# Another order of loads, scans and decode beside the first token tile, and a fifth decay buffer

## The chip, the cores and the metric

The kernel runs on one core of a Trainium2 chip. The metric is the device time of one execution in microseconds. The core has five engines with a queue of instructions each: TensorE (PE in the profile, with PEld for its weight loads), VectorE (DVE), ScalarE (ACT), GpSimd (POOL) and SyncE (SP), which here issues every transfer. Each engine takes its own queue in order.

## What is computed

Three layers follow one another. The first is a scan attention with decays over 4 batches of 8 heads, 768 positions, head size 32 and state size 16:

```
for each chunk c:
    cum = cumsum(log a);  L = exp(cum_i - cum_j), i >= j
    y   = (C B^T * L) x  +  (C state) * exp(cum)
    state = exp(sum log a) * state + sum_j B_j x_j exp(cum_end - cum_j)
```

Its output, as 3072 tokens of 256, goes through two feed-forward layers in float32:

```
h   = max(x w1, x w2, x w3);            x = h w_out      (256 -> 768 -> 256)
out = (sigmoid(x w_gate) * (x w_val)) w_out2             (256 -> 1536 -> 256)
```

## The kernel before

**Attention.** Chunks have 96 positions. A chunk is 8 *steps* (k = 8c + g) of four (batch, head) units; 32 units make 8 steps, so there are 64 steps. A step multiplies C and B (tile s, L320 in the first 16 steps, L323 behind), multiplies the result by the decays (tile mt: odd steps and the first four on VectorE, L335; even ones copied by ScalarE, L331, and multiplied on GpSimd, L332), puts B times the last decay beside it (GpSimd, L328) and multiplies by x (tile y, L341), which gives the output and the new state at once. Every fourth step, ScalarE casts y into xt_hi (L350), VectorE takes the remainder as xt_lo (L352) and transposes the new state into the next chunk's x (L356, four instructions).

**Decays.** One tile dec holds the decays of two steps. It is loaded by a broadcast transfer from a clipped copy in DRAM (load_decay, L255) and turned into running products by two scans on VectorE (decay, L271). Four buffers hold such tiles. So decays n serve steps 2n and 2n + 1.

**B and C from chunk 2 on** come as three bfloat16 parts (split_bc, L282): ScalarE casts, GpSimd subtracts, and twelve transfers put the parts in place.

**Weights of layer one** come as 64-bit words in twelve *pieces*, two for each of six column groups (a00, a01, a10, ... are pieces 0, 1, 2, ...). Decode (L152) makes float32 of a piece and splits it: three operations on ScalarE (L164 to L167), t_a and r_a on VectorE (L171, L173), a cast on ScalarE (L199) and a subtraction on GpSimd (L201). The table BEHIND says how many pieces are loaded right behind the decays of a number.

**Token tiles.** Layer one works on tiles of 512 tokens. The first needs steps 0 to 11 (START = 12). Each of its six groups makes three products u in three PSUM banks (L390 to L392; L391 reads xt_lo), whose maximum ScalarE and VectorE take (L457, L459, L461), and then the products o of the group before. Between the groups, 12 more steps of attention are fed in.

**Order.** The instructions are traced by generators in a Pipe, whose ticks fix the program's order; a planner then lays each engine's queue, by program order among what its own timing model holds ready. `issue_after(i)` adds an edge that keeps an instruction behind i on i's engine. What sets the order around the change is prepare(k) (L361), which is called in step k and issues loads, scans and the parts of the split, and the lines from L486 on.

Of the kernel before, what the change touches and what calls it, by code (L numbers as in the profile page):

```python
# [8 lines left out]
F32 = mybir.dt.float32  # L9
# [6 lines left out]
ALU = mybir.AluOpType  # L16
# [3 lines left out]
CH = 96  # L20
NC = S // CH
NU = NB * NH
NG = NU // 4
# [9 lines left out]
LW = CH + 1  # L33
PU = 8
NP = NU // PU

BW = 4 * 128
# [6 lines left out]
MASKED = 8  # L44
LEAD = 2
MTS = 5
DECS = 4
UNTIL = [12, 24, 36, 50, 64, 64, 64]
SLOT = {1: 0, 2: 1, 6: 3, 5: 4, 7: 6, 3: 2, 4: 5}
WEIGHT = {1: 0, 2: 2, 3: 1, 4: 3, 5: 4, 6: 5, 7: 6}  # L50

BEHIND = {4: 1, 5: 1, 6: 2, 7: 2, 8: 2, 9: 1, 10: 1, 11: 1, 12: 1}


class Pipe:
# [15 lines left out]
def scan_attention_then_ffn(ctx: ExitStack, tc: tile.TileContext, xh, ah, bch, pick, bn, w1, w2, w3,  # L71
# [62 lines left out]

    todo = [(piece1, m, part) for m in range(M1) for part in range(2)]
    loaded = []

    sgs = [stp.tile([128, DEC // 128, 128], I32, tag=f"sg{k}", bufs=1, name=f"sg{k}") for k in range(2)]
    blocks_done = []
    for sg in sgs:  # L140
        pool.memset(sg, 0)

    def load_weights():

        f, m, part = todo.pop(0)
        wpool, blocks, loads, name = f(m, part)
        raw = wpool.tile([128, 2 * len(loads), 128, 2], I32, tag=name, name=f"raw_{name}")
        for k, s in enumerate(loads):
            sp.dma_start(out=raw[:, 2 * k:2 * k + 2].rearrange("p b n t -> p b (n t)"), in_=s)
        loaded.append((raw, wpool, blocks, name))  # L150

    def decode(raw, wpool, blocks, name):  # L152
        nb = raw.shape[1]
        second = name[0] != "a"

        def behind(k):
            return tc.issue_after(evict[k].ins) if second else ExitStack()

        f1 = raw[..., 1]
        r = stp.tile([128, DEC // 128, 128], I32, tag="r", bufs=3, name=f"r_{name}")[:, 0:nb]  # L160
        sg = sgs[len(blocks_done) % len(sgs)][:, 0:nb]
        blocks_done.append(name)
        with behind(0):
            act.activation(out=sg.bitcast(F16).rearrange("p b (n t) -> p b n t", t=2)[..., 1], in_=f1.bitcast(F32),  # L164
                           func=AF.Identity, scale=2.0 ** -112)
            act.mul(f1.bitcast(F32), f1.bitcast(F32), 2.0 ** -112)
            act.mul(r, raw[..., 0].bitcast(U32), 2.0 ** -29)  # L167
        yield
        t = stp.tile([128, DEC // 128, 128], I32, tag="t", bufs=2, name=f"t_{name}")[:, 0:nb]
        with behind(1):  # L170
            dve.scalar_tensor_tensor(out=t, in0=f1, scalar=3, in1=sg, op0=ALU.logical_shift_left,  # L171
                                     op1=ALU.bitwise_or)
            dve.tensor_tensor(out=r, in0=t, in1=r, op=ALU.add)  # L173
        yield
        if second:
            hi, lo = store2(wpool, blocks, name)
            parts = [(r.bitcast(F32), slice(0, 4))]
            if name[0] != "d":
                v = r.bitcast(F32)
                q = wq[0].tile([128, 3, 128], F32, tag="q", name=f"q_{name}")  # L180
# [20 lines left out]
        pool.tensor_tensor(out=w[:, 1], in0=r.bitcast(F32), in1=w[:, 0].bitcast(F32),  # L201
                           op=ALU.subtract)

    def weights_tick(last=True):
        if loaded and last:
# [14 lines left out]
    def constants():  # L220
# [4 lines left out]
        for r in range(4):  # L225
# [8 lines left out]
        act.copy(delta, delta_s)  # L234

    dec, xs, cs, bx = {}, {}, {}, {}

# [16 lines left out]

    def load_decay(n, src):  # L255
        t = awk.tile([128, PU, LW], F32, tag="dec", bufs=DECS, name=f"dec{n}")
        i = sp.dma_start(out=t.rearrange("p u w -> p (u w)"), in_=src[n].partition_broadcast(128))
        dec[n] = t
        for _ in range(BEHIND.get(n, 0)):
            with tc.issue_after(i.ins):  # L260
                load_weights()

    def load_x(c, part=slice(0, NU)):
        if c not in xs:
            xs[c] = awk.tile([128, NU, D], F32, tag="xs", name=f"xs{c}")
            bx[c] = awk.tile([128, NU, N], F32, tag="bx", name=f"bx{c}")
        for t, src, n in ((xs[c], xh, D), (bx[c], bn, N)):
            sp.dma_start(out=t[:, part].rearrange("i u d -> i (u d)"),
                         in_=src[:, c, n * part.start:n * part.stop])

    def decay(n, clip=False):  # L271

# [9 lines left out]
    def split_bc(c):  # L282

        r = awk.tile([128, BW + 384], F32, tag="bc", bufs=1, name=f"bc{c}")
        sp.dma_start(out=r, in_=bch[:, c])
        parts = awk.tile([128, 3, BW + 384], BF16, tag="parts", bufs=1, name=f"parts{c}")
        cs[c] = awk.tile([KT, NU, CH], BF16, tag="cs", name=f"cs{c}")
        yield
        for p in range(3):
            with tc.issue_after(evict[0].ins) if c > 2 else ExitStack():  # L290
# [10 lines left out]
            yield splits if p == 2 else None  # L301

    steps = [(c, g) for c in range(NC) for g in range(NG)]
    done = [0]
    evict = [None, None]
    splits = []
    last = [None]

    def attention(k, ahead):

# [1 line left out]
        m = mt[k % MTS]  # L312
        if k < FIRST:
            ck = cm[:, k % MASKED]
            act.mul(ck.rearrange("p q i -> p (q i)"), bcf[c][:, BW:], pk[:, g:g + 1])
# [12 lines left out]
        pool.tensor_tensor(out=m[:, :, CH:CH + N], in0=bx[c][:, 4 * g:4 * g + 4, :],  # L328
                           in1=dc[:, :, CH:LW].to_broadcast([128, 4, N]), op=ALU.mult)
        if k >= 4 and k % 2 == 0:  # L330
            act.copy(m[:, :, 0:CH], ps[:, :, 0:CH])  # L331
            pool.tensor_tensor(out=m[:, :, 0:CH], in0=m[:, :, 0:CH], in1=dc[:, :, 1:LW],  # L332
                               op=ALU.mult)
        else:
            last[0] = dve.tensor_tensor(out=m[:, :, 0:CH], in0=ps[:, :, 0:CH], in1=dc[:, :, 1:LW],  # L335
                                        op=ALU.mult)
        prepare(k)
        yield
        y = ys[g // 4]
# [3 lines left out]
        if g % 4 == 3:  # L343
# [6 lines left out]
            act.copy(hi, src)  # L350
            yield
            dve.tensor_tensor(out=lo, in0=src, in1=hi.bitcast(F32), op=ALU.subtract)  # L352
            if c + 1 < NC:
                for q in range(4):
                    rows = slice(32 * q, 32 * q + 32)
                    dve.transpose(  # L356
                        out=xs[c + 1][rows, 16 * h:16 * h + 16, :].rearrange(
                            "p (g q) d -> p g q d", q=4)[:, :, q, :],
                        in_=y[rows, :, CH:128])

    def prepare(k):  # L361

        c, g = divmod(k, NG)
        if g == 0 and 0 < c < NC - 1:
            load_x(c + 1)
            splits.append(split_bc(c + 1))
        if splits and next(splits[0], None) is splits:
            splits.pop()
        n = k // 2
        if k % 2 == 0:  # L370
            if 5 <= n + 4 < NC * NP:
                load_decay(n + 4, ad)
        elif k < 9:
            decay(n + 1, n == 0)
        else:
            for i in ([n + 1] if k == 9 else []) + [n + 2]:
                if i < NC * NP:
                    with tc.issue_after(last[0].ins) if k > FIRST else ExitStack():
                        decay(i)

    def att_step(ahead=0):
# [365 lines left out]
```

## Time and profile before

| | us |
|---|---|
| median of 3 runs | 570.01 (569.87 to 570.12) |
| the profiled execution | 567.58 |
| its span, first to last instruction | 565.7 |
| TensorE busy | 535.5 (95%) |
| VectorE busy | 402.8 (71%) |
| ScalarE busy | 318.9 (56%) |
| GpSimd busy | 179.0 (32%) |

All rows are of that one profiled execution; times are counted from the start of its span. A duration is one instruction's, and pipelined instructions overlap. An "idle before" names the engine or transfer that ended the idle time. PEclk is the clock that TensorE was granted, as a share of full speed.

### The profile page before, as it was taken

The numbers are of one execution on the slowest core, as the hardware profiler recorded it, in microseconds if no ns is written. First come the engines' busy times: TensorE is split into PE (matmuls) and PEld (weight loads), VectorE is DVE, ScalarE is ACT, GpSimd is POOL, SyncE is SP. The second block draws the span as 40 slices with busy tenths as digits, with TensorE's granted clock in tenths as the row PEclk, the third lists the DMA queues.
The fourth block names the chain that finished last, engine by engine and source line by source line (L and its number), as shares of the span: only waits on it lengthen the run. The fifth ranks groups of instructions, "written<-read, shape, count | busy, mean of one in ns | idle before, by whom it ended". The sixth has DMA issues, their size and how long they took to land.

```text
span 565.7 us, 7988 instructions
## 1 busy us (share of the span) xinstructions
PE 535.5 (95%) x2885; PEld 421.3 (74%) x2885; DVE 402.8 (71%) x620; ACT 318.9 (56%) x568; POOL 179.0 (32%) x201
## 2 busy tenths in 40 slices
PE   5778899999999999999999999999999999999996
PEld 4556667677777778887677776878888888788885
DVE  4899986666866735899988887696555567555555
ACT  5776735334334324677586776466555565555553
POOL 3667956454655423657522322000000000000000
PEclk9859899999999999999999999999999999999999
DMA  7999975894986018014120000002000002000002
GB/s 255 340 282 233 241 161 117 183 173 130 195 200 122 30 49 323 1 37 137 52 75 0 2 1 2 0 0 75 0 1 0 2 1 75 0 1 0 1 0 75
DMA packets 32007, 50.52 MB, mean 89 GB/s; under 512 B 3168, under 2 KB 17888, under 8 KB 31968
## 3 DMA queue, kind: packets, MB, share of 16 engines
q1 hardware_dynamic: 31968, 50.02, 33.8%
q8 instruction: 22, 0.36, 0.3%
q14 instruction: 17, 0.14, 0.1%
HBM read 38.51 MB, written 3.25 MB: 74 GB/s over the span
## 4 chain that ended last, share of the span: by engine, by line
PE 65%; DVE 20%; DMA 5%; ACT 4%; issue 4%; SPq 1%; DVEq 0%; ACTq 0%
PE o L629 14%; PE ug L595 12%; PE uv L595 12%; PE u L390 6%; PE u L391 6%; PE u L392 6%; PE y L341 2%; PE o L390 2%; PE o L391 2%; PE o L392 2%; DMA cs<-parts 2%; DVE t_v L171 2%; PE s L323 1%; DVE dec L279 1%; DVE lo L669 1%
## 5 line engine op out<-in xcount | busy, mean ns | idle before, releaser
L629 PE MATMUL o<-hi,w_d 128*128 128x512 f32 x288 | 97.2, 390 | 0.0
L390 PE MATMUL u<-xt_hi,w_a 128*128 128x512 f32 x216 | 89.5, 415 | 3.8 <-DVE s L461 2.0
L595 PE MATMUL uv<-xt_hi,w_v 128*128 128x512 f32 x252 | 90.8, 392 | 2.3 <-DVE s L461 1.7
L595 PE MATMUL ug<-xt_hi,w_g 128*128 128x512 f32 x252 | 90.9, 390 | 1.4 <-ACT y L614 1.4
L391 PE MATMUL u<-xt_lo,w_a 128*128 128x512 f32 x216 | 86.1, 399 | 1.8 <-DVE xt_lo L352 1.8
L392 PE MATMUL u<-xt_hi,w_a 128*128 128x512 f32 x216 | 85.7, 397 | 0.0
L669 DVE TENSOR_TENSOR lo<-y,hi 128x512 fp32r<-128x512 f32 x72 | 52.7, 733 | 16.7 <-ACT hi L668 15.8
L452 POOL TENSOR_TENSOR lo<-s,hi 128x512 fp32r<-128x512 f32 x36 | 50.8, 1410 | 43.2 <-ACT hi L450 43.2
L629 PEld LDWEIGHTS o<-hi,w_d 128*128 128x128 f32 x288 | 53.9, 188 | 11.5 <-ACT hi L668 0.6
L279 DVE TENSOR_TENSOR_SCAN dec<-dec,delta 128x388 f32<-128x388 f32 x64 | 57.9, 944 | 2.0 <-DMA dec<-ad 1.8
L595 PEld LDWEIGHTS uv<-xt_hi,w_v 128*128 128x128 f32 x252 | 47.3, 188 | 15.0 <-DVE s L461 2.1
L629 PE MATMUL o<-lo,w_d 128*128 128x512 f32 x144 | 56.7, 394 | 1.6 <-DVE lo L669 1.6
L595 PEld LDWEIGHTS ug<-xt_hi,w_g 128*128 128x128 f32 x252 | 47.3, 188 | 12.4 <-issue 1.8
L390 PEld LDWEIGHTS u<-xt_hi,w_a 128*128 128x128 f32 x216 | 41.4, 191 | 16.6 <-DVE s L461 2.8
L450 ACT CAST hi<-s 128x512 fp32r<-128x512 f32 x36 | 22.3, 619 | 54.1 <-DVE s L461 53.7
L665 DVE TENSOR_TENSOR y<-uv,y 128x512 f32<-128x512 f32 x36 | 24.8, 688 | 34.8 <-PE uv L595 32.8
L595 PE MATMUL uv<-xt_lo,w_v 128*128 128x512 f32 x126 | 49.1, 389 | 0.0
L595 PE MATMUL ug<-xt_lo,w_g 128*128 128x512 f32 x126 | 49.1, 389 | 0.0
L391 PEld LDWEIGHTS u<-xt_lo,w_a 128*128 128x128 f32 x216 | 41.4, 192 | 9.9 <-DVE xt_lo L352 2.3
L392 PEld LDWEIGHTS u<-xt_hi,w_a 128*128 128x128 f32 x216 | 41.4, 192 | 9.2
L668 ACT CAST hi<-y 128x512 fp32r<-128x512 f32 x72 | 44.4, 619 | 5.6 <-DVE y L665 5.6
L607 DVE TENSOR_TENSOR y<-ug,y 128x512 f32<-128x512 f32 x36 | 24.8, 689 | 19.7 <-ACT y L602 12.8
(103 smaller groups left out, 976.7 us busy)
## 6 DMA issues: line engine op xcount, KB each, us to landing
dec<-ad SPq DMA_DIRECT2D x30, 388.0 KB, 5.7
raw_a<-in_w SPq DMA_DIRECT2D x18, 256.0 KB, 6.2
bi<-parts SPq DMA_DIRECT2D x36, 128.0 KB, 6.1
cs<-parts SPq DMA_DIRECT2D x36, 96.0 KB, 6.4
xs<-in_xh SPq DMA_DIRECT2D x6, 512.0 KB, 5.3
raw_g<-in_wg SPq DMA_DIRECT2D x6, 512.0 KB, 5.1
raw_v<-in_wv SPq DMA_DIRECT2D x6, 512.0 KB, 6.0
raw_d<-in_wo SPq DMA_DIRECT2D x6, 512.0 KB, 3.4
```

Source lines behind the costliest of these rows:

```text
L279: dve.tensor_tensor_scan(out=f, data0=f, data1=delta.rearrange("p u w -> p (u w)"), initial=0.0, op0=ALU.mult, op1=ALU.add)
L390: pe.matmul(ps, wlo, a_hi(k), start=k == 0, stop=False)
L391: pe.matmul(ps, whi, a_lo(k), start=False, stop=False)
L392: pe.matmul(ps, whi, a_hi(k), start=False, stop=k == kn - 1)
L450: act.copy(hl[0], s)
L452: eng.tensor_tensor(out=hl[1], in0=s, in1=hl[0].bitcast(F32), op=ALU.subtract)
L595: pe.matmul(ps, w, x, start=new and e == 0, stop=e == 2, skip_group_check=not new)
L607: evict[1] = dve.tensor_tensor(out=self.t[k], in0=ps, in1=self.t[k], op=ALU.add)
L629: pe.matmul(acc2[t][d], w, x, start=n == 1 and e == 0, stop=n == M2 and e == 2)
L665: evict[1] = dve.tensor_tensor(out=g, in0=v, in1=g, op=ALU.mult)
L668: act.copy(hl[0], g)
L669: dve.tensor_tensor(out=hl[1], in0=g, in1=hl[0].bitcast(F32), op=ALU.subtract)
```

## The change

The fifth buffer for decays and the table of the weights' places:

```
+HELD = (START // 2, START // 2 + 1)
-DECS = 4
+DECS = 5
-BEHIND = {4: 1, 5: 1, 6: 2, 7: 2, 8: 2, 9: 1, 10: 1, 11: 1, 12: 1}
+BEHIND = {5: 2, 6: 2, 8: 2, 9: 2, 10: 2, 11: 1, 12: 1}
```

Up to step 12, loads of decays, x and weights are issued in the program's order, each behind the last one issued:

```
+    def in_turn():
+        return tc.issue_after(issued[-1].ins) if issued and len(done) and done[0] <= START \
+            else ExitStack()
```

Decode of pieces 0 and 1 stands behind work of the steps (begun), that of pieces 2 and 3 behind the last xt_hi and xt_lo ahead of the tile (opened):

```
         def behind(k):
-            return tc.issue_after(evict[k].ins) if second else ExitStack()
+            if second:
+                return tc.issue_after(evict[k].ins)
+            if n < 2:
+                return tc.issue_after(begun[n][k].ins)
+            return tc.issue_after(opened[k].ins) if n < 4 else ExitStack()
...
+        with behind(2) if n < 2 else ExitStack():
+            pool.tensor_tensor(out=w[:, 1], in0=r.bitcast(F32), in1=w[:, 0].bitcast(F32),
+                               op=ALU.subtract)
```

begun[0] is: ScalarE's xt_hi of step 3, VectorE's product of step 7, GpSimd's product of step 10; begun[1] is: ScalarE's copy of step 10, VectorE's product of step 9, GpSimd's product of step 10. ScalarE's multiplications of C (L315) of steps from 1 on stand behind the copy of delta.

The scans of decays 6 and 7 (HELD), the transposes of step 7 and the start of chunk 2's split stand behind the xt_lo of step 11:

```
+            low = dve.tensor_tensor(out=lo, in0=src, in1=hi.bitcast(F32), op=ALU.subtract)
+            if k == START - 1:
+                opened[:] = high, low
+                with tc.issue_after(low.ins):
+                    decay(HELD[0])
+                    late.pop()()
+                    decay(HELD[1])
+                next(splits[0])
+            if k == NG - 1:
+                late.append(lambda: turn(c, h, y))
+            elif c + 1 < NC:
+                turn(c, h, y)
```

turn is the four transposes, as before. In prepare, loads of x and of B and C come behind the decays (for chunk 2, x stays ahead), and the scans stand behind the step's product on VectorE from step 5 on, where before this held from step 17 on:

```
-        if g == 0 and 0 < c < NC - 1:
+        if k == NG:
             load_x(c + 1)
-            splits.append(split_bc(c + 1))
-        if splits and next(splits[0], None) is splits:
+        if splits and opened and next(splits[0], None) is splits:
             splits.pop()
...
                 load_decay(n + 4, ad)
+            if g == 0 and 0 < c < NC - 1:
+                with tc.issue_after(issued[-1].ins):
+                    if k > NG:
+                        load_x(c + 1)
+                    load_bc(c + 1)
         elif k < 9:
-            decay(n + 1, n == 0)
+            with tc.issue_after(last[0].ins) if k > 3 else ExitStack():
+                decay(n + 1, n == 0)
         else:
             for i in ([n + 1] if k == 9 else []) + [n + 2]:
-                if i < NC * NP:
-                    with tc.issue_after(last[0].ins) if k > FIRST else ExitStack():
+                if i < NC * NP and i not in HELD:
+                    with tc.issue_after(last[0].ins):
                         decay(i)
```

load_bc issues the load of B and C, which split_bc did itself before; the casts of chunk 2's split stand behind opened[0]. The first loads stand in this order:

```
     sp.dma_start(out=pk, in_=pick)
-    sp.dma_start(out=bcf[0][:, BW:], in_=bch[:, 0, BW:])
     store_all = clip_all()
     next(store_all)
+    sp.dma_start(out=bcf[0][:, BW:], in_=bch[:, 0, BW:])
+    load_decay(0, ah)
     sp.dma_start(out=bcf[0][:, 0:BW], in_=bch[:, 0, 0:BW])
-    load_decay(0, ah)
...
     load_decay(1, ah)
+    load_x(0, slice(16, 32))
+    issued.append(sp.dma_start(out=bcf[1], in_=bch[:, 1]))
     load_decay(2, ad)
-    load_x(0, slice(16, 32))
-    sp.dma_start(out=bcf[1], in_=bch[:, 1])
```

## Rows read from the trace of the kernel before

**Rows 1.** Stretches of the span: length, busy time of each engine (instructions), clock, DMA.

```profile
20.00:76.46 56.46, 45.11 (x307) 33.57 (x305) 53.13 (x75) 42.69 (x77) 42.52 (x43) 0.82 1.02 253
76.46:566.00 489.54, 477.81 (x2473) 376.62 (x2473) 338.74 (x530) 265.67 (x473) 129.44 (x133) 1.00 0.24 62
...
11.22:72.98 61.76, 50.19 (x377) 37.93 (x377) 58.63 (x83) 43.69 (x77) 43.63 (x47) 0.83 1.02 274
38.39:72.98 34.59, 30.71 (x196) 22.68 (x197) 33.59 (x43) 24.60 (x43) 28.59 (x25) 0.90 0.99 242
62.93:72.98 10.05, 9.44 (x76) 6.71 (x75) 9.78 (x9) 4.92 (x9) 9.58 (x9) 1.00 1.11 202
```

**Rows 2.** Timeline of TensorE: start, duration, instruction, idle time before.

```profile
38.44 0.80 PE L391 MATMUL u<-xt_lo,w_a 128*128 128x512 f32 x1 [1.77 <-DVE xt_lo L352]
...
55.35 0.40 PE L341 MATMUL y<-mt,xs 128*32 128x112 f32 x8 [1.63 <-DVE mt L335]
...
57.87 0.50 PE L390 MATMUL u<-xt_hi,w_a 128*128 128x512 f32 x1 [1.59 <-DVE s L461]
...
82.10 0.50 PE L390 MATMUL u<-xt_hi,w_a 128*128 128x512 f32 x1
```

**Rows 3.** Timeline of VectorE.

```profile
19.75 1.81 DVE L279 TENSOR_TENSOR_SCAN dec<-dec,delta 128x388 f32<-128x388 f32 x2 [1.00 <-DMA dec<-ad]
22.32 1.81 DVE L279 TENSOR_TENSOR_SCAN dec<-dec,delta 128x388 f32<-128x388 f32 x2 [0.76 <-DMA dec<-ad]
...
27.50 1.81 DVE L279 TENSOR_TENSOR_SCAN dec<-dec,delta 128x388 f32<-128x388 f32 x2
...
32.95 1.28 DVE L356 STREAM_TRANSPOSE xs<-y 32x128 f32<-32x128 f32 x4
34.26 1.23 DVE L171 SCALAR_TENSOR_TENSOR t_a<-raw_a,sg 128x512 int32<-128x512 int32 x1
35.52 1.81 DVE L279 TENSOR_TENSOR_SCAN dec<-dec,delta 128x388 f32<-128x388 f32 x2
37.25 0.67 DVE L173 CUSTOM_DVE_ANT_0 r_a<-t_a,r_a 128x1024 uint16<-128x1024 uint16 x1
37.84 0.55 DVE L352 TENSOR_TENSOR xt_lo<-y,xt_hi 128x384 fp32r<-128x384 f32 x1
...
63.54 1.50 DVE L171 SCALAR_TENSOR_TENSOR t_a<-raw_a,sg 128x512 int32<-128x512 int32 x1
65.18 2.17 DVE L173 CUSTOM_DVE_ANT_0 r_a<-t_a,r_a 128x1024 uint16<-128x1024 uint16 x1
...
70.06 1.66 DVE L171 SCALAR_TENSOR_TENSOR t_a<-raw_a,sg 128x512 int32<-128x512 int32 x1
71.85 1.21 DVE L173 CUSTOM_DVE_ANT_0 r_a<-t_a,r_a 128x1024 uint16<-128x1024 uint16 x1
```

**Rows 4.** Timeline of ScalarE.

```profile
21.17 0.78 ACT L164 ACTIVATE sg<-raw_a 128x512 f16<-128x512 f32 x1 [1.02 <-DMA raw_a<-in_w]
...
33.12 0.47 ACT L350 CAST xt_hi<-y 128x384 fp32r<-128x384 f32 x1
```

**Rows 5.** Waits of SyncE's queue before 80 us: total, times, longest.

```profile
SPq L257 <- DVE mt L335: 11.9, 4, 4.4
```

**Rows 6.** Timeline of SyncE's issues.

```profile
2.60 0.43 SPq L257 DMA_DIRECT2D dec<-in_ah  x1
...
11.85 0.61 SPq L285 DMA_DIRECT2D bc<-in_bch  x1
12.90 0.33 SPq L257 DMA_DIRECT2D dec<-ad  x1
```

**Rows 7.** Stretch 18.00 to 38.39, GpSimd's subtractions of the split (L300) alone.

```profile
18.00:38.39 20.39, 3.78 (x2) 0.66 1.07 294
```

**Rows 8.** VectorE from 8 to 76 us by form: busy, mean ns, idle before.

```profile
L173 DVE CUSTOM_DVE_ANT_0 r_a<-t_a,r_a 128x1024 uint16<-128x1024 uint16 x11 | 12.9, 1179 | 0.8 <-ACT mt L331 0.6
L171 DVE SCALAR_TENSOR_TENSOR t_a<-raw_a,sg 128x512 int32<-128x512 int32 x12 | 12.5, 1042 | 1.4 <-ACT raw_a L166 1.3
```

More of the change, by code (lines that the diff above doesn't have):

```diff
@@ L136, in scan_attention_then_ffn @@
     loaded = []
+    issued = []
+    def in_turn():
+        return tc.issue_after(issued[-1].ins) if issued and len(done) and done[0] <= START \
+            else ExitStack()
     sgs = [stp.tile([128, DEC // 128, 128], I32, tag=f"sg{k}", bufs=1, name=f"sg{k}") for k in range(2)]
     blocks_done = []
+    begun, opened = [[None] * 4, [None] * 4], []
+    done = []
     for sg in sgs:
@@ L148, in load_weights @@
         for k, s in enumerate(loads):
-            sp.dma_start(out=raw[:, 2 * k:2 * k + 2].rearrange("p b n t -> p b (n t)"), in_=s)
+            issued.append(sp.dma_start(
+                out=raw[:, 2 * k:2 * k + 2].rearrange("p b n t -> p b (n t)"), in_=s))
         loaded.append((raw, wpool, blocks, name))
@@ L154, in decode @@
         second = name[0] != "a"
+        n = len(blocks_done)
         def behind(k):
-            return tc.issue_after(evict[k].ins) if second else ExitStack()
+            if second:
[3 more added lines that the diff above has]
+            return tc.issue_after(opened[k].ins) if n < 4 else ExitStack()
         f1 = raw[..., 1]
@@ L200, in decode @@
         yield
-        pool.tensor_tensor(out=w[:, 1], in0=r.bitcast(F32), in1=w[:, 0].bitcast(F32),
-                           op=ALU.subtract)
+        with behind(2) if n < 2 else ExitStack():
+            pool.tensor_tensor(out=w[:, 1], in0=r.bitcast(F32), in1=w[:, 0].bitcast(F32),
+                               op=ALU.subtract)
     def weights_tick(last=True):
@@ L233, in constants @@
             pool.memset(d[:, r, 0:1], 1.0)
-        act.copy(delta, delta_s)
+        begun[0][3] = act.copy(delta, delta_s)
     dec, xs, cs, bx = {}, {}, {}, {}
@@ L256, in load_decay @@
         t = awk.tile([128, PU, LW], F32, tag="dec", bufs=DECS, name=f"dec{n}")
-        i = sp.dma_start(out=t.rearrange("p u w -> p (u w)"), in_=src[n].partition_broadcast(128))
+        with in_turn():
+            i = sp.dma_start(out=t.rearrange("p u w -> p (u w)"),
+                             in_=src[n].partition_broadcast(128))
+        issued.append(i)
         dec[n] = t
@@ L267, in load_x @@
         for t, src, n in ((xs[c], xh, D), (bx[c], bn, N)):
-            sp.dma_start(out=t[:, part].rearrange("i u d -> i (u d)"),
-                         in_=src[:, c, n * part.start:n * part.stop])
+            with in_turn():
+                issued.append(sp.dma_start(out=t[:, part].rearrange("i u d -> i (u d)"),
+                                           in_=src[:, c, n * part.start:n * part.stop]))
     def decay(n, clip=False):
@@ L280, in decay, with load_bc, split_bc @@
                                    initial=0.0, op0=ALU.mult, op1=ALU.add)
-    def split_bc(c):
+    def load_bc(c):
         r = awk.tile([128, BW + 384], F32, tag="bc", bufs=1, name=f"bc{c}")
         sp.dma_start(out=r, in_=bch[:, c])
+        splits.append(split_bc(c, r))
+    def split_bc(c, r):
         parts = awk.tile([128, 3, BW + 384], BF16, tag="parts", bufs=1, name=f"parts{c}")
@@ L289, in split_bc @@
         for p in range(3):
-            with tc.issue_after(evict[0].ins) if c > 2 else ExitStack():
+            with tc.issue_after((evict[0] if c > 2 else opened[0]).ins):
                 act.copy(parts[:, p], r)
@@ L303, in scan_attention_then_ffn @@
     steps = [(c, g) for c in range(NC) for g in range(NG)]
-    done = [0]
+    done.append(0)
     evict = [None, None]
@@ L307, in scan_attention_then_ffn @@
     last = [None]
+    late = []
     def attention(k, ahead):
@@ L314, in attention @@
             ck = cm[:, k % MASKED]
-            act.mul(ck.rearrange("p q i -> p (q i)"), bcf[c][:, BW:], pk[:, g:g + 1])
+            with tc.issue_after(begun[0][3].ins) if k else ExitStack():
+                act.mul(ck.rearrange("p q i -> p (q i)"), bcf[c][:, BW:], pk[:, g:g + 1])
         ps = psu.tile([128, 4, 128], F32, tag="up", name=f"s{c}_{g}")
@@ L330, in attention @@
         if k >= 4 and k % 2 == 0:
-            act.copy(m[:, :, 0:CH], ps[:, :, 0:CH])
-            pool.tensor_tensor(out=m[:, :, 0:CH], in0=m[:, :, 0:CH], in1=dc[:, :, 1:LW],
-                               op=ALU.mult)
+            copy = act.copy(m[:, :, 0:CH], ps[:, :, 0:CH])
+            product = pool.tensor_tensor(out=m[:, :, 0:CH], in0=m[:, :, 0:CH],
+                                         in1=dc[:, :, 1:LW], op=ALU.mult)
+            if k == START - 2:
+                begun[1][0] = copy
+                begun[0][2] = begun[1][2] = product
         else:
@@ L336, in attention @@
                                         op=ALU.mult)
+        if k == 7:
+            begun[0][1] = last[0]
+        if k == 9:
+            begun[1][1] = last[0]
         prepare(k)
@@ L349, in attention, with turn @@
                       for v in (xt_hi, xt_lo))
-            act.copy(hi, src)
+            high = act.copy(hi, src)
+            if k == 3:
+                begun[0][0] = high
             yield
[L352 to L359, printed above, removed]
+            low = dve.tensor_tensor(out=lo, in0=src, in1=hi.bitcast(F32), op=ALU.subtract)
[10 more added lines that the diff above has]
+                turn(c, h, y)
+    def turn(c, h, y):
+        for q in range(4):
+            rows = slice(32 * q, 32 * q + 32)
+            dve.transpose(
+                out=xs[c + 1][rows, 16 * h:16 * h + 16, :].rearrange(
+                    "p (g q) d -> p g q d", q=4)[:, :, q, :],
+                in_=y[rows, :, CH:128])
     def prepare(k):
         c, g = divmod(k, NG)
-        if g == 0 and 0 < c < NC - 1:
+        if k == NG:
             load_x(c + 1)
-            splits.append(split_bc(c + 1))
-        if splits and next(splits[0], None) is splits:
+        if splits and opened and next(splits[0], None) is splits:
             splits.pop()
```

## The prediction, made before the changed kernel was run

> **What bounds the kernel now.** I read the stretches first [rows 1]. From 76.46 us on, TensorE is busy 477.81 of 489.54 us at a granted clock of 1.00 (the 2.4 GHz level), so what lies behind is bound by TensorE's own work, and a gain ahead of 76 us simply moves all of it. From 20.00 to 76.46 it is busy only 45.11 of 56.46 us, at a mean clock of 0.82. The reader is to see in the same group which engine is full there: VectorE works 58.63 of the 61.76 us from 11.22 to 72.98, and 33.59 of the 34.59 us from 38.39 on. In the longer stretch it is idle for 61.76 - 58.63 = 3.13 us in all. TensorE's idle places lead to it [rows 2]: the first product with xt_lo starts at 38.44 after 1.77 us of waiting for xt_lo, then come 1.63 us for a product of attention and 1.59 us for a maximum, all three made by VectorE.
>
> The queue of VectorE ahead of the first token tile shows the order that the change is about [rows 3]. ScalarE has written xt_hi of step 11, the last that the tile needs, at 33.12 + 0.47 = 33.59 [rows 4]. VectorE's answer, xt_lo, starts at 37.84. In between stand the four transposes of chunk 0's second half (1.28), t_a of piece 2 (1.23), the two scans of decays 7 (1.81) and r_a of piece 2 (0.67); the two scans of decays 6 (1.81) lie further ahead, at 27.50. None of these feeds step 11 or the first weights.
>
> **The change part by part.** *Held scans, late transposes, pieces 2 and 3.* They leave the queue ahead of xt_lo: 1.81 + 1.28 + 1.23 + 1.81 + 0.67 = 6.80 us [rows 3]. If all that stood ahead moves up by as much, the first tile opens at 38.44 - 6.80 = 31.6; if xt_hi stays at 33.59, the gain is the 37.84 - 33.59 = 4.25 us that xt_lo waited. So the opening moves by 4.3 to 6.8 us. But the same 6.80 us, and the transposes of step 11 with them, now stand right behind xt_lo on VectorE, ahead of the maxima of the first groups (L459, L461), which give TensorE its PSUM banks back. VectorE was full from there on already. So the opening by itself is a loan: what was done before 38.4 is done after 31.6, and the tile ends when VectorE has worked off its list. Its value is between 0 and 6.8 us; I take 0, because the row nearest to it [rows 1] has one idle microsecond in 34.59.
>
> *What is not a loan* is idle time of VectorE that goes away: at most the 3.13 us. The scans of decays 4 and 5 wait 1.00 and 0.76 us for their transfers [rows 3]. The rest, 1.37 us, lies in small pieces between the steps and ahead of the opening, where an order that serves the steps first has work to put.
>
> *The fifth buffer and the order of SyncE's queue.* SyncE waited 11.9 us in four places for a product before it could issue a decay into one of four buffers [rows 5], and its queue is in order, so the weights behind it waited too. The fifth buffer lets each go two steps earlier. Chunk 2's B and C (448 KB, issued at 11.85) stood ahead of decays 4 (12.90) [rows 6]; now they go behind decays 8. That place alone is 12.90 - 11.85 = 1.05 us, against the 1.00 that decays 4 were late, and the second half of chunk 1's x and B, which also stood ahead, comes on top. Decays 5 now go ahead of piece 0 and its 512 KB, so their 0.76 us go too. I count both waits as gone; at the other bound, with the transfers as late as now, 1.76 of the 3.13 us stay. ScalarE waited 1.02 us for piece 0, until 21.17 [rows 4], with the steps' copies queued behind; now it may start a piece only behind xt_hi of step 3, so late weights hold up fewer copies.
>
> The new order adds waits too. On SyncE's queue, decays 8, 9 and 10 wait for the products of steps 7, 9 and 11, with pieces 4 to 9 behind them; those pieces are decoded behind the opening and the products lie ahead of it, so this costs nothing unless the opening slips. On VectorE the scans of decays 5 now stand behind the product of step 9, so that product, the scans (1.81), the product of step 11, its y (0.40 as in [rows 2]) and its xt_hi (0.47) are in series. While y and xt_hi run, 0.40 + 0.47 = 0.9 us, VectorE has decode of piece 1 and an earlier xt_lo to do: the cost is 0 to 0.9 us, and I take 0.3, since r_a alone (0.67, its lowest in [rows 3]) fills most of it.
>
> *The split of chunk 2* (three casts on ScalarE, two subtractions on GpSimd, twelve transfers) moves behind the opening. GpSimd did the two subtractions ahead of 38.39 in 3.78 us [rows 7]. From 38.39 to 72.98 it is busy 28.59 of 34.59 us, so there is room for 3.78, but not for much more; ScalarE has 24.60 of 34.59 and takes the casts without cost. Decode on VectorE, though, depends on what GpSimd does beside it: all scans take 1.81 us a pair, but t_a and r_a have means of 1042 and 1179 ns [rows 8] and go from 0.67 to 2.17 [rows 3]. The pieces decoded ahead of the opening lose GpSimd's subtractions as neighbours, those behind gain them. At best three pieces fall from the mean of 2.22 to twice the lowest 0.67, 3 x (2.22 - 1.34) = 2.6 us less; at worst it is the third rival's price. I take 0, for the neighbour only changes places.
>
> The Trainium skill ("SBUF — State Buffer", section "Who interferes with whom") says that a VectorE instruction with two SBUF inputs and a GpSimd instruction that reads SBUF shut each other out, each for the whole length of the other. The trace agrees in form: t_a and r_a have two such inputs and spread by a factor of three, the scans read one operand from PSUM and do not spread. By that rule a fuller GpSimd behind the opening makes decode dearer there, which is the third rival.
>
> *The rest* (the order of ScalarE's first multiplications, decays 0 one place earlier on the queue, which is 0.43 us of issue in [rows 6]): between 0 and 0.4 us gained at the very start; I take 0, since the scans of decays 1 still wait for their own transfer. In the later tiles only the place of x, B and C behind the decays changes; TensorE is idle there for 489.54 - 477.81 = 11.73 us, spread thin, and I count no change.
>
> **Sum.** -3.13 + 0.3 = -2.8 us. The profiled execution took 567.58 us (span 565.7), so 564.8 by its own time, with a span of 562.9. The median of the runs shown is 570.01, 2.4 above the profiled one; I carry that over: 567.2. With the transfers as late as now the gain is 2.8 - 1.76 = 1.0, with decode 2.6 cheaper it is 5.4, so this case runs from 564.6 to 569.0.
>
> **The rivals.** *First: part of the loan is kept.* VectorE does some work ahead of need: r_a of piece 10 ends at 71.85 + 1.21 = 73.06 [rows 3], while the group that uses it starts on TensorE at 82.10 [rows 2]. If it is such work that slides, its t_a and r_a (1.66 + 1.21) come on top of the idle time: 3.13 + 2.87 = 6.0 us, and 6.8 with the whole opening kept. That is 570.01 - 6.0 = 564.0, or 563.2 at the far end. For it: TensorE lost more than VectorE ever gave back in this stretch, 56.46 - 45.11 = 11.35 us and the half clock besides, so it could follow. Against it: decode stands early in the program and takes its turn before the maxima, now as before.
>
> *Second: nothing comes of it.* The DMA engines' mean share from 20.00 to 76.46 is 1.02 [rows 1]. If the total of the transfers paces the stage, decays come earlier only to make the weights later, and VectorE waits for those: 570.0, with the 0.3 us added 570.3. Against it: the 11.9 us in which SyncE issued nothing.
>
> *Third: slower, through GpSimd.* The subtractions and the low parts of the weights crowd together behind the opening, and decode meets them there. From 62.93 to 72.98 GpSimd is busy 9.58 of 10.05 us [rows 1], and pieces 9 and 10 cost VectorE 1.50 + 2.17 and 1.66 + 1.21, a mean of 3.27 us a piece, where the mean of all is 1.04 + 1.18 = 2.22. If the seven pieces 2 to 8 paid 3.27 as well, 7 x 1.05 = 7.4 us would come on top: 574.6. The gain is used up from 2.8 / 7 = 0.4 us a piece on; slower by over 0.2% needs 3.9 / 7 = 0.56; halfway, at 0.53, it is 570.9. Against it: 3.78 us are a ninth of the stretch, and a ninth of the 3.27 - 1.34 that a piece pays there at most is 0.21 a piece.
>
> **How the numbers follow.** About 0.2%, 1.1 us, is what a measurement of this kernel can tell from no change. I give the forecast 0.50, the first rival 0.25, the second 0.13, the third 0.12. Forecast and first rival are faster, but for 0.01 at the forecast's upper edge, which goes to the same: 0.74. The second rival is the same: 0.14 with that edge. The third, as far as it passes 0.56 us a piece, with any other delay of this size behind the opening: 0.12. The range goes from the far end of the first rival, 563.2, to just past the second, 570.6, which leaves most of the third and a little of the first out.
>
> **What would show it.** Right: xt_lo of step 11 starts within a microsecond after its xt_hi, and the first product with it comes at 31 to 34 us; the scans of decays 4 and 5 no longer wait for a transfer; VectorE has no idle time from the opening to the maxima of the fourth group; TensorE's steady stretch begins some 2.8 us before 76.46. Wrong: the steady stretch begins over 5 us earlier (first rival); SyncE's waits are gone but ScalarE waits longer for raw weights than now (second); t_a and r_a together take 2.6 us or more in the mean, or the first product of step 16 waits for the parts of chunk 2 (third, or a price that I did not count).

## The result, and the profile after

The changed kernel takes 575.66 us (median of 4 runs, 575.02 to 575.72), the kernel before 569.94 beside it (4 runs, 568.35 to 570.12). The ratio is 1.0107, 95% interval 1.0088 to 1.0125: slower by 5.7 us, outside the predicted range. One execution of E3 below (579.55 us) and one of E12 (583.77) ran longer at a lower granted clock; they are left out, and with E12's its trace.

| | us |
|---|---|
| the profiled execution | 575.72 |
| its span | 573.7 |
| TensorE busy | 537.4 (94%) |
| VectorE busy | 404.7 (71%) |
| ScalarE busy | 320.2 (56%) |
| GpSimd busy | 178.0 (31%) |

The spans of the two profiled executions differ by 8.0 us, the medians by 5.7. Where does the time go? The end of the first token tile is a good mark, ScalarE's last copy of its output. ScalarE's timeline, before and after:

```profile
92.39 1.07 ACT L409 COPY y<-o 128x512 f32<-128x512 f32 x2 [0.75 <-PE o L392]
```

```profile
98.69 1.08 ACT L461 COPY y<-o 128x512 f32<-128x512 f32 x2 [0.75 <-PE o L444]
```

So 6.3 us are lost ahead of this mark and 1.7 behind it. The profiled execution of the kernel before was a short one, though, 2.4 us under its median. E10 below turned out to be the same program, with the same instructions in the same order on every engine, and its profiled execution took 570.18 us (span 568.1). Its copy, its first product with xt_lo, and its stretch that answers to the third in [rows 1]:

```profile
94.81 1.08 ACT L409 COPY y<-o 128x512 f32<-128x512 f32 x2 [0.75 <-PE o L392]
41.05 0.79 PE L391 MATMUL u<-xt_lo,w_a 128*128 128x512 f32 x1
11.22:72.98 61.76, 54.80 (x353) 42.63 (x353) 56.16 (x82) 43.95 (x77) 42.73 (x46) 0.97 0.98 269
```

So what one execution shows ahead of the mark can be 2.4 us off: against E10's, 3.9 us are lost ahead of it and 1.7 behind. TensorE's timeline after:

```profile
32.09 0.80 PE L442 MATMUL u<-xt_hi,w_a 128*128 128x512 f32 x1 [3.08 <-POOL w_a L216]
32.68 0.63 PE L443 MATMUL u<-xt_lo,w_a 128*128 128x512 f32 x1
...
57.41 0.74 PE L442 MATMUL o<-hi,w_a 128*128 128x512 f32 x2 [2.08 <-ACT hi L502]
58.99 0.79 PE L443 MATMUL o<-lo,w_a 128*128 128x512 f32 x1 [0.85 <-POOL lo L504]
59.59 0.63 PE L444 MATMUL o<-hi,w_a 128*128 128x512 f32 x1
60.01 0.63 PE L443 MATMUL o<-lo,w_a 128*128 128x512 f32 x1
63.98 0.80 PE L348 MATMUL s<-cs,bi 96*128 96x96 bf16 x8 [2.92 <-DMA cs<-parts]
...
168.31 0.50 PE L348 MATMUL s<-cs,bi 96*128 96x96 bf16 x8 [1.45 <-DMA dec<-ad]
```

The first product with xt_lo comes 5.8 us earlier than in [rows 2], half a microsecond behind the one with xt_hi: the opening moved as forecast. What TensorE waits for there is no longer xt_lo but the first weights' low part, which GpSimd makes (3.08 us); xt_lo itself came 7.8 us earlier, at 30.05 instead of 37.84. The loss comes later. The first product of step 16, the one with s<-cs,bi, waits 2.92 us for chunk 2's parts and starts at 63.98; before, it ran at 55.69. TensorE takes its queue in order, so the products behind it stand too. The head start was gone even ahead of step 16: the first product with lo (o<-lo) ran at 54.13 after the change, at 52.65 before and at 55.25 in E10. In the last line another such step, in a later chunk, waits 1.45 us, most of the 1.7 lost behind the mark. The profile puts this wait down to a transfer of decays, which the step does not read; the last parts that it does read landed at 167.96, 0.35 us ahead of its start.

The stretches after (length; PE, PEld, DVE, ACT, POOL busy; clock; DMA share; GB/s), three of them with a partner in [rows 1]:

```profile
11.22:72.98 61.76, 46.20 (x332) 34.80 (x331) 58.14 (x80) 44.10 (x77) 38.82 (x43) 0.81 0.90 260
20.00:76.46 56.46, 41.69 (x285) 30.35 (x284) 53.17 (x74) 42.26 (x73) 39.92 (x40) 0.79 0.87 239
...
55.22:62.93 7.71, 2.92 (x7) 1.46 (x6) 7.33 (x13) 6.94 (x12) 4.25 (x4) 0.69 1.07 281
62.93:72.98 10.05, 8.14 (x44) 5.78 (x45) 8.91 (x10) 6.87 (x13) 7.62 (x7) 0.56 0.21 57
```

From 55.22 to 62.93 TensorE is busy only 2.92 of 7.71 us. From 62.93 to 72.98 its granted clock is 0.56, near the 1.2 GHz level, where [rows 1] had 1.00: in this last stretch it is busy 8.14 us for 44 matmuls, against 9.44 for 76. The DMA share there is 0.21 against 1.11. VectorE's idle time from 11.22 to 72.98 is 61.76 - 58.14 = 3.62 us; in the kernel before it was 3.13 in one execution and 61.76 - 56.16 = 5.60 in E10's.

SyncE's queue shows the chain of chunk 2, from the load of its B and C to its last two transfers of parts. Before (the load, at 11.85, is in [rows 6]):

```profile
47.08 0.56 SPq L296 DMA_DIRECT2D bi<-parts  x1
47.74 0.80 SPq L296 DMA_DIRECT2D cs<-parts  x1
```

After:

```profile
29.91 0.34 SPq L304 DMA_DIRECT2D bc<-in_bch  x1
...
58.23 0.56 SPq L319 DMA_DIRECT2D bi<-parts  x1
58.84 0.60 SPq L319 DMA_DIRECT2D cs<-parts  x1
```

The transfer issued at 47.74 landed 5.9 us later, at 53.67, which is 2.0 us ahead of the first use at 55.69; in E10's execution the slack was 6.9 us. After the change the one issued at 58.84 landed 5.1 us later, at 63.94, just when step 16 starts. SyncE then stood itself. Its waits before 80 us, which answer to [rows 5] (total, times, longest):

```profile
SPq L273 <- DVE mt L363: 12.3, 3, 10.4
```

The four waits for a decay's buffer are three, but the total is not smaller: one of 10.4 us lies between 60 and 70.65, when the next decays wait for a product on VectorE (mt, at 69.87) that stands behind the late step 16 and, from 62.55 to 69.83, behind decode. That is why the DMA engines have so little to do from 62.93 on.

ScalarE's three casts of chunk 2's chain ran at 18.70, 22.36 and 26.73 before. After:

```profile
41.77 0.91 ACT L314 CAST parts<-bc 128x896 bf16<-128x896 f32 x1
...
47.29 0.93 ACT L314 CAST parts<-bc 128x896 bf16<-128x896 f32 x1
...
57.26 0.94 ACT L314 CAST parts<-bc 128x896 bf16<-128x896 f32 x1
```

Before, the last cast was done at 27.65 and the last transfers left only at 47.08 and 47.74; they left within 1 us of it after the change. The load landed at 37.46, so the casts did not follow at once: the third stood in ScalarE's queue behind a cast of weights that waited 2.51 us for r_a on VectorE.

VectorE after the change, the xt_lo of step 11, and the two operations of a decoded piece from 8 to 76 us, which answer to [rows 8]:

```profile
30.05 0.55 DVE L386 TENSOR_TENSOR xt_lo<-y,xt_hi 128x384 fp32r<-128x384 f32 x1
...
L187 DVE CUSTOM_DVE_ANT_0 r_a<-t_a,r_a 128x1024 uint16<-128x1024 uint16 x12 | 13.5, 1140 | 0.5
L185 DVE SCALAR_TENSOR_TENSOR t_a<-raw_a,sg 128x512 int32<-128x512 int32 x12 | 13.1, 1097 | 0.8 <-ACT raw_a L180 0.7
```

A piece costs 1.14 + 1.10 = 2.24 us, before 2.22. Decode did not get dearer.

### The profile page after: what moved, and what is told of

Same layout as the page of the kernel before. It is cut to its first block, busy times and chain, and to the rows that moved or that the text cites. A ratio compares the mean times of both kernels' runs of the same rounds, so it can differ in the third digit from the quotient of the medians.

```text
span 573.7 us, 7979 instructions
## 1 busy us (share of the span) xinstructions
PE 537.4 (94%) x2885; PEld 421.8 (74%) x2885; DVE 404.7 (71%) x620; ACT 320.2 (56%) x568; POOL 178.0 (31%) x201
## 4 chain that ended last, share of the span: by engine, by line
PE 63%; DVE 16%; DMA 10%; ACT 5%; issue 3%; SPq 1%; POOL 0%; DVEq 0%; ACTq 0%
PE o L681 15%; PE ug L647 12%; PE uv L647 12%; PE u L442 6%; PE u L443 5%; PE u L444 5%; DMA dec<-ad 4%; DMA raw_a<-in_wo 3%; PE y L373 2%; DMA raw_a<-in_w 2%; PE o L442 2%; PE o L443 2%; DVE t_v L185 2%; PE o L444 2%; PE s L348 1%
## 5 line engine op out<-in xcount | busy, mean ns | idle before, releaser
L442 PE MATMUL u<-xt_hi,w_a 128*128 128x512 f32 x216 | 90.6, 419 | 6.6 <-POOL w_a L216 3.1
L444 PE MATMUL u<-xt_hi,w_a 128*128 128x512 f32 x216 | 86.4, 400 | 0.0
```

What stands on the lines that cost most here:

```text
L442: pe.matmul(ps, wlo, a_hi(k), start=k == 0, stop=False)
L444: pe.matmul(ps, whi, a_hi(k), start=False, stop=k == kn - 1)
```

## The experiments

The theory after this reading: two parts of the change cost more than the rest brings, the late split of chunk 2, and the place of the later chunks' x, B and C behind the decays. The rivals: VectorE is full and the early opening disturbs it; or the held work, the fifth buffer or the decode do. Every ratio is to the kernel before, timed beside it (its medians there 569.72, 569.28 and 569.26), with its 95% interval.

**E1: chunk 2's load and split early again.** In the changed kernel:

```
-        if splits and opened and next(splits[0], None) is splits:
+            load_bc(c + 1)                       # still under k == NG
+        if splits and next(splits[0], None) is splits:
...
-            if g == 0 and 0 < c < NC - 1:
+            if g == 0 and 1 < c < NC - 1:        # x, B, C behind the decays
...                                               # the start of the split at the opening goes,
                                                  # and no cast stands behind opened[0]
```

> The changed kernel, with chunk 2's load of B and C and its split let free again as before; all else of the change stays. Theory 1 (the late split): TensorE's stall ahead of step 16 (2.92 us for the parts, with 2.08 and 0.85 before it) and the half clock behind it go; the first product of step 16 runs at 53 to 57 us instead of 63.98, and the time is 566 to 570. Theory 2 (the loan: scans of decays 6 and 7 and two rounds of transposes behind the opening hold up the maxima): the stall only changes its name, 573 to 576. Theory 3 (decode dearer beside GpSimd): with two subtractions fewer behind the opening 1 to 2 us come back, 573 to 575.

572.72 us, 1.0045 (1.0024 to 1.0066): over half of the loss is gone, and the time lies above the 566 to 570 expected. Step 16 starts at 53.06. TensorE's timeline of E1 shows that start and what is late next:

```profile
53.06 0.50 PE L348 MATMUL s<-cs,bi 96*128 96x96 bf16 x8 [0.60 <-DMA raw_a<-in_w]
...
72.82 0.33 PE L348 MATMUL s<-cs,bi 96*128 96x96 bf16 x4 [1.70 <-DVE s L510]
...
76.46 0.80 PE L441 MATMUL u<-xt_hi,w_a 128*128 128x512 f32 x1 [2.12 <-DVE s L512]
...
166.26 0.50 PE L348 MATMUL s<-cs,bi 96*128 96x96 bf16 x8 [1.70 <-DMA dec<-ad]
```

Of step 16's wait 0.60 us are left; the profile names a transfer of weights, but the last parts landed at 52.92. The next two wait for maxima, the last is the wait in the later chunk again. VectorE's timeline of E1 tells why the maxima are late:

```profile
72.09 0.68 DVE L510 TENSOR_TENSOR s<-u,s 128x512 f32<-128x512 f32 x1
72.69 1.78 DVE L185 SCALAR_TENSOR_TENSOR t_a<-raw_a,sg 128x512 int32<-128x512 int32 x1
74.61 1.20 DVE L187 CUSTOM_DVE_ANT_0 r_a<-t_a,r_a 128x1024 uint16<-128x1024 uint16 x1
75.73 0.68 DVE L512 TENSOR_TENSOR s<-u,s 128x512 f32<-128x512 f32 x1
```

Between two maxima of one group stand t_a and r_a of the last piece.

**E2: the late split alone, in the kernel before.** Chunk 2's B and C behind decays 8, its casts behind the last xt_hi of step 11:

```
+            if c > 1:
+                load_bc(c + 1)
...
+                if k == NG:
+                    with tc.issue_after(i.ins):  # i: the load of decays 8
+                        load_bc(c + 1)
```

> The kernel before, with one part of the change alone: chunk 2's B and C are loaded behind decays 8 and split behind the xt_hi of step 11. Theory 1: step 16's first product waits for parts and comes at 62 us or later (now 55.69); 574 to 578. Theory 2: the held scans are not held here, so the time stays within 1 us of 570. Theory 3: 571 to 573.

581.92 us, 1.0199 (1.0169 to 1.0228): by itself it costs 11 to 12 us, more than expected. The chain is later still (load at 36.13, last parts issued at 60.99), and so is step 16. TensorE's timeline of E2, and under it the stretch of E2 that had 0.56 after the change, with the long one:

```profile
64.32 0.79 PE L404 MATMUL o<-lo,w_a 128*128 128x512 f32 x1 [5.56 <-POOL lo L465]
...
68.30 0.82 PE L329 MATMUL s<-cs,bi 96*128 96x96 bf16 x8 [1.90 <-DMA bc<-in_bch]
```

```profile
62.93:72.98 10.05, 6.75 (x22) 4.97 (x23) 4.26 (x5) 5.36 (x9) 7.44 (x8) 0.51 0.61 138
...
11.22:72.98 61.76, 43.70 (x302) 33.70 (x302) 50.45 (x78) 41.52 (x73) 37.55 (x42) 0.75 0.85 243
```

The last parts landed at 68.25, 0.05 us ahead of step 16's start, though the profile names the next chunk's load. Standing and half clock come together here too. The stop spreads: VectorE, full in [rows 1], is busy only 50.45 of 61.76 us, with waits of 3.8 and 1.9 us for ScalarE's part of decode. And GpSimd has the split's second subtraction (57.01) and two of weights (59.32) in its queue ahead of the lo (63.01) for which TensorE waits 5.56 us.

**E3: load early, casts late.** The changed kernel, chunk 2's B and C loaded where E1 loads them, the casts kept behind xt_hi of step 11:

```
-                next(splits[0])
+                for _ in range(4):
+                    next(splits[0])
+                splits.pop()
...
+            load_bc(c + 1)                       # under k == NG
```

> The changed kernel, with chunk 2's B and C loaded at an early free place in SyncE's queue, but the casts still behind the xt_hi of step 11. Theory 1, if the late transfer is what matters (it landed at about 36, the first cast ran at 41.77): the first cast starts at 30 to 33, the last transfers are issued some 17 us later, at 47 to 50, step 16 runs at 54 to 57: 566 to 571. If the place behind the opening is what matters, 573 to 576 as now.

572.52 us, 1.0040 (1.0018 to 1.0061), the same as E1; the casts and step 16 come earlier than expected, the time does not. ScalarE's timeline of E3 shows the first and the last cast, and TensorE's shows step 16 on time, with no wait:

```profile
28.68 0.94 ACT L314 CAST parts<-bc 128x896 bf16<-128x896 f32 x1
...
39.47 0.93 ACT L314 CAST parts<-bc 128x896 bf16<-128x896 f32 x1
```

```profile
53.33 0.34 PE L348 MATMUL s<-cs,bi 96*128 96x96 bf16 x4
```

So it is not the rule that the casts stand behind xt_hi: with the data there they follow at once. In the changed kernel the load stands at 29.91 behind decays 8, and the casts, the subtractions and the transfers all follow from that.

**E4: E1, and the later chunks' loads ahead of the decays again,** their split starting in the same step, as before:

```
-        if k == NG:
+        if g == 0 and 0 < c < NC - 1:
             load_x(c + 1)
+            load_bc(c + 1)
...
-            if g == 0 and 0 < c < NC - 1:
-                with tc.issue_after(issued[-1].ins):
-                    ...
```

> As the first of these four, and the loads of x, B and C of the later chunks stand ahead of the decays again. In the changed kernel one step waits 1.45 us at 168.31 for the parts of a later chunk, whose B and C were loaded behind decays and x. Theory 1: that wait goes too, 1 to 2 us below the first of the four (565 to 569). Otherwise the same as that one.

567.81 us, 0.9964 (0.9947 to 0.9982): faster than before by 0.4%. What is left of the change (opening, held work, fifth buffer, the first loads) brings 2.1 us. The wait near 166 us is gone. ScalarE's copy and TensorE's first product with xt_lo in E4:

```profile
92.08 1.07 ACT L456 COPY y<-o 128x512 f32<-128x512 f32 x2 [1.11 <-PE o L439]
```

```profile
34.63 0.63 PE L438 MATMUL u<-xt_lo,w_a 128*128 128x512 f32 x1
```

The opening is 38.44 - 34.63 = 3.8 us earlier than before and the tile's end 0.3; against E10's execution of the program before they are 6.4 and 2.7 earlier. Either way the larger part, 3.5 or 3.7 us, is taken back inside the tile. In E4 piece 11's t_a stands behind both maxima:

```profile
72.90 0.69 DVE L508 TENSOR_TENSOR s<-u,s 128x512 f32<-128x512 f32 x1
...
76.17 1.35 DVE L185 SCALAR_TENSOR_TENSOR t_a<-raw_a,sg 128x512 int32<-128x512 int32 x1
```

**E9: E1, with the split of the later chunks started in the step of its load** (one `next(splits[0])` behind load_bc), the loads still behind the decays:

> The first kernel (E1: the change with chunk 2's split early), where x, B and C of later chunks stay behind the decays, but the split starts in the same step as before, not one later. It tells the two halves of that edit apart. If the lost step makes the parts late: the wait of 1.70 us at 166 goes and the time is 568 to 571 (E1 572.7, E4 567.8). If the place behind the decays in SyncE's queue does: within 0.7 us of E1.

570.95 us, 1.0018 (1.0004 to 1.0031). The wait near 166 us is gone. From E1 to E4 the later loads cost 1.0045 - 0.9964 = 0.0081, or 4.6 us; the step lost is about 1.5 of it (the intervals of E1 and E9 overlap, but the wait that went was 1.70 us), and the place behind the decays the other 3.1. The last pieces' decode stands ahead of the maxima in E1 and E9 and not in E4; that it is the cause of these 3.1 us is likely, and no run separates it.

**E8: the later loads behind the decays, alone, in the kernel before:**

```
-        if g == 0 and 0 < c < NC - 1:
+        if k == NG:
...
+                if g == 0 and 1 < c < NC - 1:
+                    with tc.issue_after(i.ins):  # i: the load of decays
+                        load_x(c + 1)
+                        load_bc(c + 1)
```

> The kernel before, with another part of the change alone: from chunk 3 on, x and B and C are loaded behind the decays and the split starts a step later. In the changed kernel, the first and the third of these experiments TensorE waits 1.4 to 1.7 us for a later chunk's parts, and E4, which undoes just this, is 4.9 us faster than the first. Theory 1 (late parts, whatever the chunk): 2 to 5 us slower than before, 572 to 575, with a wait of 1 us or more at a first product of a later step (L323 of before). Otherwise within 0.7 us of before, and E4's gain over the first is something else.

586.29 us, 1.0293 (1.0270 to 1.0316): 17 us, far above what was expected. SyncE's queue and TensorE in E8:

```profile
112.27 13.49 SPq L257 DMA_DIRECT2D dec<-ad  x2
...
126.76 0.68 SPq L286 DMA_DIRECT2D bc<-in_bch  x1
```

```profile
118.71 0.48 PE L331 MATMUL s<-cs,bi 96*128 96x96 bf16 x4 [3.92 <-DMA cs<-parts]
...
175.68 0.80 PE L331 MATMUL s<-cs,bi 96*128 96x96 bf16 x8 [4.03 <-DMA dec<-ad]
```

The line of 13.49 us holds two loads of decays with a wait between them: for 12.6 us SyncE waits for a product on VectorE (mt). The next chunk's B and C leave behind it.

**E12: only the later loads ahead, chunk 2's split late:**

```
-        if k == NG:
+        if g == 0 and 0 < c < NC - 1:
             load_x(c + 1)
+            if c > 1:
+                load_bc(c + 1)
```

> The changed kernel, where only the later chunks' x, B and C stand ahead of the decays again and their split starts in the same step; chunk 2's split stays late. With E1 and E4 it closes the square: if the two costs are separate, late split 3.5 us and late loads 4.9, the time is 575.7 - 4.9, that is 570 to 572, with the wait for chunk 2's parts still at step 16 and none for a later chunk's. If one hides the other: 573 to 576.

574.44 us, 1.0078 (1.0060 to 1.0096). Only its time is used. It fills the square (us against the kernel before, by the ratios):

| | later loads behind | later loads ahead |
|---|---|---|
| split of chunk 2 late | +6.1 (after) | +4.4 (E12) |
| split of chunk 2 early | +2.6 (E1) | -2.1 (E4) |

The split costs 3.5 or 6.5 us and the loads 1.7 or 4.7; each hides some 3 us of the other, and the two together cost 8.2. The 1.7 alone is not clear of the measurement: those intervals overlap. By the medians the four are +5.7, +5.2, +3.0 and -1.9, which gives the split 2.7 or 7.1 us, the loads 0.5 or 4.9, and both together 7.6.

**E5: E4 without the held scans and late transposes; E6: E4 with four buffers.**

```
-                with tc.issue_after(low.ins):    # E5
-                    decay(HELD[0])
-                    late.pop()()
-                    decay(HELD[1])
...
-DECS = 5                                         # E6
+DECS = 4
```

> The fourth kernel (E4: the change with the splits and loads of B and C placed as before), with the scans of decays 6 and 7 and the transposes of step 7 back in their old places ahead of the opening. If the earlier opening is a loan that VectorE takes back (E4 opened at 31.9 instead of 38.4 and still ended the first tile at 92.1 instead of 92.4): the opening slips to 34 to 36 and the tile ends within 1 us of E4's, time 567 to 569. If the earlier opening is worth something by itself: 2 us or more slower than E4, 570 to 572.

> E4 with four buffers for decays instead of five. If SyncE's waits for a free buffer cost what the prediction said (two scans late by 1.00 and 0.76 us, weights behind them late too): 1.5 to 3 us slower, 569 to 571. If the transfers' total paces the stage whatever their order: within 0.7 us of E4.

E5: 568.54 us, 0.9992 (0.9974 to 1.0011). E6: 569.71, 1.0008 (0.9991 to 1.0026). The fifth buffer is worth 0.0044, some 2.5 us, in E4; holding 0.0028, 1.6 us, with intervals that overlap. E5's first product with xt_lo comes at 32.83, earlier than E4's, so holding is not what opens the tile early.

**E7: E4, with less decode ahead of the maxima.** Pieces from the fifth on enter later, in every second slot of the first tile:

```
-    for _ in range(9):
+    for n in range(9):
...
-        weights_tick()
+        weights_tick(n < 4)
...
-        weights_tick(t < NTT - 2 or s % 4 == 3)
+        weights_tick(s % 2 == 0 if t == 0 else t < NTT - 2 or s % 4 == 3)
```

**E10** makes that edit alone in the kernel before, **E11** makes it in E5.

> E4 with pieces 4 and on entering decode one every second slot of the first tile instead of all ahead of it, so that VectorE's maxima and products come ahead of decode that is not yet needed. If it is this order that takes the loan back (TensorE waits 2.09 and 1.44 us for maxima at 54.55 and 66.26 in E4): the first tile ends 2 to 5 us earlier, 563 to 566. If VectorE's sum alone binds: within 1 us of E4. If decode then comes late for TensorE: waits for w_a (L216) in the third group on, 569 or more.

> The kernel before, with decode of pieces 4 and on entering one every second slot of the first tile, and nothing of the change. If the order of decode ahead of the maxima was what TensorE paid for in this stage also before the change (waits of 1.63, 1.59 and 0.96 us): 2 to 4 us faster, 565 to 567.5. If it needs the earlier opening to have room: within 0.7 us of before.

> The seventh kernel (E7, 565.3: all loads and splits of B and C as before, decode later) without the held scans and the late transposes. If holding is worth nothing (as in the fifth, 568.5 beside 567.8): within 1 us of E7. If holding pays once decode no longer takes the loan back: 2 us or more slower, 567.5 to 569.

E7: 565.31 us, 0.9925 (0.9906 to 0.9943), the best version here, ahead of both kernels and 0.0039, 2.2 us, ahead of E4. E10: 569.39, 0.9999 (0.9980 to 1.0019). E11: 568.84, 0.9991 (0.9966 to 1.0016). These two say nothing of the edit. The queues of E10 hold the same instructions in the same order as those of the kernel before, on every engine, and those of E11 the same as E5's: the planner laid what it lays without the edit. E7's queues do differ from E4's. So E10 and E11 are second measurements of two programs, and what later decode would bring in the kernel before, or without holding, stays open. From E5 to E7, holding and later decode together bring 0.0067, 3.8 us. ScalarE's copy and the long stretch in E7:

```profile
90.71 1.07 ACT L456 COPY y<-o 128x512 f32<-128x512 f32 x2
```

```profile
11.22:72.98 61.76, 50.19 (x390) 37.63 (x390) 58.83 (x91) 46.20 (x83) 43.17 (x48) 0.89 0.99 283
```

VectorE is as busy as in E4 (58.83 us, there 58.73), so in these two executions its idle time hardly differs. Two things do: the order of its list, and the price of a piece. Its r_a from 8 to 80 us, in E4 and then in E7:

```profile
L187 DVE CUSTOM_DVE_ANT_0 r_a<-t_a,r_a 128x1024 uint16<-128x1024 uint16 x12 | 12.5, 1048 | 0.9
L187 DVE CUSTOM_DVE_ANT_0 r_a<-t_a,r_a 128x1024 uint16<-128x1024 uint16 x12 | 11.3, 949 | 0.7
```

With t_a (1070 and 1055 ns) a piece costs 2.12 us in E4 and 2.00 in E7, which over twelve pieces is 1.4 of the 2.2 us. No run separates the order from the cheaper pieces.

## Why the prediction was wrong

*Opening: right.* The product with xt_lo starts at 32.68, inside 31 to 34, and half a microsecond behind xt_hi's. That it is a loan was right too, as long as decode keeps its place: E4 gives back 3.5 of 3.8 us, or 3.7 of 6.4.

*The step that failed: the split of chunk 2.* "Now they go behind decays 8. That place alone is 12.90 - 11.85 = 1.05 us" took the later place of B and C for pure gain, and "there is room for 3.78" and "takes the casts without cost" took the late split for free. GpSimd and ScalarE did have room; it was not the question. The chain is load, casts, subtractions, transfers, landing, and in the kernel before it ended 2 to 7 us ahead of its use: last parts issued at 47.74, landed at 53.67, used at 55.69 (6.9 us of slack in E10's execution). I had not read that row. Moving the chain's head by 29.91 - 11.85 = 18.1 us was far more than that slack. The chain itself got 7.0 us shorter (before the change its finished parts had stood in SyncE's queue for 19 us), and its last issue still came 11.1 us later. The prediction's last sentence named this as "a price that I did not count", and it is 3.5 to 6.5 us (E1 and E12 against the square).

*The later chunks: wrong.* "I count no change" is 1.7 to 4.7 us. The step that the split starts later shows as a wait of 1.45 us in the changed kernel and 1.70 in E1; the rest goes together with the last pieces' decode ahead of the maxima, which no run separates.

*VectorE's 3.13 us: wrong.* The waits for decays 4 and 5 went, as forecast, but others came, most of them at the front. VectorE's timeline after:

```profile
11.70 0.56 DVE L294 TENSOR_SCALAR dec<-dec 128x768 f32<-128x768 f32 x1 [1.78 <-DMA dec<-in_ah]
15.70 1.81 DVE L298 TENSOR_TENSOR_SCAN dec<-dec,delta 128x388 f32<-128x388 f32 x2 [0.68 <-DMA dec<-ad]
20.64 0.56 DVE L363 TENSOR_TENSOR mt<-s,dec 128x384 f32<-128x384 f32 x1 [0.49 <-PE s L345]
```

Of the first wait, 0.48 us lie behind 11.22. In E4, with the chain in place, VectorE is idle 61.76 - 58.73 = 3.03 us. Since the same program shows 3.13 us in one execution and 5.60 in another, it can't be told whether E4's 2.1 us are idle time taken away. The forecast carried the 2.4 us between the profiled execution and the median over as if they lay apart from this idle time; in E10's execution they lie in it, with one wait of 2.91 us at 34.13.

*SyncE's waits: half right.* Until 60 us they fell from 4.4 to 1.9 us in all, but 10.4 came back behind step 16. In E7 the total before 80 us is 2.7.

*The rivals.* The third had the sign; its mechanism is false (2.24 us a piece against 2.22). The first, decode ahead of need that slides, may be what E7 gains by once the rest is in place; that E7 comes within 1.5 us of that rival's time does not show it. The second is false for this change: the time did not stay, and from 20.00 to 76.46 the DMA share fell from 1.02 to 0.87.

*Open:* why each of the two parts costs far more in the kernel before (11 to 12 us and 17) than in the change. E2's trace answers in part: the stop reached VectorE and GpSimd's queue. With four buffers SyncE's queue stands longer (the 12.6 us of E8), but no run separates that.

## What to carry to other kernels

An operation moved because its engines have room takes its whole chain along: read from the trace when the chain's last transfer lands and when it is first used, and compare that slack with the move. An in-order engine turns one late operand into a stop of everything behind it. Where an engine is full, starting its consumer earlier is a loan until the work behind the start is ordered by need. Where a planner lays the queues, an edit can vanish in it: compare the queues before you believe that an edit brings nothing. And one profiled execution can lie 2.4 us off the median, as much as the gains that are looked for here.

## What was not expected of the hardware

TensorE's granted clock was 0.56 from 62.93 to 72.98, the 1.2 GHz level for most of it; the same stretch of E2, in which waits of 5.56 and 1.90 us end, had 0.51. At that level products of the first layer start 0.43 us apart, at the other level 0.23. The clock fell ahead of the long wait: after those of 2.08 and 0.85 us the products at 59.59 and 60.01 are 0.42 us apart already, and the wait of 2.92 us came behind them. What the half clock cost is open. The program of the kernel before ran from 11.22 to 72.98 at a mean clock of 0.83 in one execution and at 0.97 in the other, and the one at 0.97 had the longer span, by 2.4 us: there the clock did not decide which was faster.
